# Issuing a branch's transfers from GpSimd instead of SyncE, and storing one of the two split output chunks whole

## The chip, the cores and the metric

The kernel runs on one core of a Trainium2 chip. Its engines are TensorE (PE; its weight loads are PEld), VectorE (DVE), ScalarE (ACT), GpSimd (POOL) and SyncE (SP). A q behind a name (SPq, POOLq) is that engine's sequencer, which waits, branches and issues transfers. The metric is the device time of one execution in microseconds (us), less is better. Before the change the median of three runs is 294.77 us (294.74 to 294.92).

## What is computed

```
x   = attention(q, k, v, s)          # 8 batches, 8 heads, 576 positions, width 64
#     scores = q k^T / 8 + min(-(cum_i - cum_j), 0), causal, softmax; cum = cumsum(max(s, 0))
h   = relu(x^T w_tok1) w_tok2        # token mixing, 576 -> 256 -> 576
u   = x + h^T
out = u + relu(u w_ch1) w_ch2        # channel mixing, 512 -> 1536 -> 512; float32
```

## The kernel before

The fast path assumes that the inputs stay in a range in which the softmax needs no row maximum. While it runs it computes a flag that says whether this held (`flagi`, line 1364). At its end all five engines load the flag (line 1399) and branch on it (line 1402). Where the flag is 0, as with these inputs, they jump over `general`, a slow and safe version of the whole computation in a loop over the batches; the profile has no row of `general`.

On the fast path the work is a list of operations with costs, priorities and dependences. A planner (`Plan.run`) walks it once, gives each operation an engine and a start, and the instructions are then written out in the order of those starts; each engine runs its own list in that order. The cores of the work per batch `b` are `quad` and `pair` (attention), `tok` (token mixing) and `chan` (channel mixing).

`chan(b, ...)` first makes `g`, the hidden layer, and then the output in chunks of 128 positions. For each chunk, 12 matmuls (line 1261) sum `wc2` against `g` into one of four accumulators `pmx`, VectorE adds `u` (line 1269) into one of four output buffers `of`, and SyncE stores it (line 1274). `whole` (line 1255) says whether a chunk is made in one piece of 512 columns or in two of 256; it is false for chunk 3 (`NJ - 2`) of the last two batches, 6 and 7. In `ga` lies the hidden layer of an even batch, in `gb` that of an odd one. The planner puts the last chunks of batch 7 (from `gb`) ahead of the last three of batch 6 (from `ga`), so that the last store of the program is one of batch 6.

Each transfer raises a semaphore when it has landed. Those issued by SyncE go round eight of them, DMAHW0 to DMAHW7, those issued by GpSimd round another eight, DMASW0 to DMASW7. Where the two sides of the branch meet again, the side that was taken must have raised every semaphore as far as the other side would have: the skipping side therefore waits for its own count on each semaphore that `general` uses and adds what `general` would have added. After that come line 1429, where SyncE waits for all engines and all sixteen queues in twelve instructions of two semaphores each (the DMASW ones first, then DMAHW0 to DMAHW7 in turn, each beside an engine's), and a closing barrier. In the profile line 1402 holds the branch and that adding up, line 1429 the closing waits, and line 1418 the opening ones.

Of the kernel before, what the change touches and what calls it, by code (L numbers as in the profile page):

```python
# [262 lines left out]
def c_pe(n, f32=False):  # L263
    occ = n * (4 if f32 else 1) / 2400.0 + 0.0025
    return occ, occ + 0.21
# [17 lines left out]
def general(ctx, tc, q, k, v, out, cum, ident, w1, w2, wc1, wc2):  # L283

    nc = tc.nc
    B, H, S, D = q.shape
    NJ, DM, NCC = 5, H * D, wc2.shape[1]
    AX = mybir.AxisListType.X
    scr = tc.dram_tile([B * H, S], FP32, name="scr")
    with tc.tile_pool(name="gen", bufs=1) as gp, tc.tile_pool(name="gen2", bufs=2) as g2, \  # L290
            tc.tile_pool(name="genp", bufs=1, space=bass.MemoryType.PSUM) as pp:
        nc.sync.dma_start(out=scr[:, :], in_=cum[:, :])
        with tc.For_i(0, B, 1) as b:
            x = gp.tile([128, NJ, DM], BF16, name="gx", tag="gx")
            alln = []
            for i, src in enumerate((q, k, v)):
                f = g2.tile([128, NJ, H, D], FP32, name="gf", tag="gf")
                nc.vector.memset(f[64:128, NJ - 1, :, :], 0.0)
                for c in range(NJ):
                    n = min(128, S - c * 128)  # L300
                    nc.sync.dma_start(
                        out=f[0:n, c, :, :],
                        in_=src[bass.ds(b, 1), :, c * 128 : c * 128 + n, :].rearrange("o h p d -> p (o h) d"))
                t = gp.tile([128, NJ, H, D], BF16, name="gn", tag=f"gn{i}")
                nc.vector.tensor_copy(out=t[:, :, :, :], in_=f[:, :, :, :])
                alln.append(t)
            cb = gp.tile([128, H, S], FP32, name="gcb", tag="gcb")
            nc.sync.dma_start(
                out=cb[:, :, :], in_=scr[bass.ds(b * H, H), :].unsqueeze(0).to_broadcast([128, H, S]))
            for h in range(H):  # L310
                nat = [t[:, :, h, :] for t in alln]
# [51 lines left out]
            for c in range(NJ):  # L363
# [7 lines left out]
                for m in range(4):  # L371
# [3 lines left out]
                                      in_=pt[:, :].rearrange("p (m t) -> p m t", m=4))  # L375
# [8 lines left out]
            for c in range(NJ):  # L384
                n = min(128, S - c * 128)
                pm = pp.tile([128, DM], FP32, name="gpm", tag="gpm")
                for cc in range(NCC):
                    nc.tensor.matmul(out=pm[:, :], lhsT=g[:, cc, c * 128 : c * 128 + 128], rhs=wc2[:, cc, :],
                                     start=(cc == 0), stop=(cc == NCC - 1))
                o = g2.tile([128, DM], FP32, name="go", tag="go")  # L390
                nc.vector.tensor_tensor(out=o[:, :], in0=pm[:, :], in1=u[:, c, :], op=ALU.add)
                nc.sync.dma_start(out=out[bass.ds(b, 1), c * 128 : c * 128 + n, :].rearrange("o p d -> (o p) d"),
                                  in_=o[0:n, :])


# [1 line left out]
def kernel(  # L397
# [12 lines left out]
    nc = tc.nc  # L410

    B, H, S, D = q.shape
# [3 lines left out]
    NJ = 5  # L416
# [17 lines left out]
    def sb(name, shape, dt, pool=None):  # L434
        return (pool or const).tile(shape, dt, name=name, tag=name)
# [124 lines left out]
    cum = sb("cum", [64, S], FP32)  # L560
# [7 lines left out]
    def dve(n, fn, two=False):  # L568
        return {"DVE": (*c_dve(n, two), fn)}
# [15 lines left out]
    for ti, src in enumerate((k, q)):  # L585
# [4 lines left out]
        for f in range(2):  # L590
            def cast0(eng, ti=ti, f=f):
# [4 lines left out]
                else:  # L596
# [9 lines left out]
        out=cum[:, :], data0=one_sb[:, 0:1].to_broadcast([64, S]), data1=s_sb[:, :], initial=0.0, op0=ALU.mult, op1=ALU.add))},  # L606
        reads=["sr"], writes=["cum"], prio=2)
    P.op(dve(1, lambda: nc.vector.tensor_scalar(
        out=half[:, :], in0=cum[:, S - 1 : S], scalar1=-0.5, scalar2=None, op0=ALU.mult)),
        reads=["cum"], writes=["half"], prio=-1)  # L610
    P.op(act(576, lambda: nc.scalar.activation(
        out=wn[:, 0:S], in_=cum[:, :], func=AF.Exp, bias=half[:, 0:1], scale=1.0), True),
        reads=["half", "cum"], writes=["wn"], prio=-5)
    P.op({"ACT": (1.0, 1.1, lambda: nc.scalar.copy(out=neg[:, :, :],
                                                   in_=zero[:, :].unsqueeze(1).to_broadcast([128, 2, 512])))},
# [602 lines left out]
    def chan(b, u, us, uT):  # L1218
        P.shift = SHIFT["chan"][b]
        odd = b % 2  # L1220
        rank = 4 * (b + 1) + LAG
        g = Buf(r_gb if odd else r_ga)
        spans = [(0, 256), (256, 640)] if b == 1 else [(0, 320), (320, 640)] if odd else [(0, 256), (256, 512)] if b == 0 else [(0, 512)]
        for (cc, (a, e)) in ([(cc, sp) for hf in range(2) for sp in spans for cc in range(6 * hf, 6 * hf + 6)] if b < 2 else
                             [(cc, sp) for cc in range(NCC) for sp in spans]):
            if True:
                ukeys = ([(uT, c, m) for c in range(2) for m in range(NMC)] if b < 1 and a == 0 else
                         [(uT, c) for c in range(a // 128, (e + 127) // 128)])
                pm = Buf(r_mx, False)
                n = e - a  # L1230

                def mm(cc=cc, pm=pm, a=a, e=e):
                    for m in range(NMC):
                        nc.tensor.matmul(out=pm.t[:, 0 : e - a], lhsT=wc1[:, m, cc * 128 : cc * 128 + 128],  # L1234
                                         rhs=uT.t[:, m, a:e], start=(m == 0), stop=(m == NMC - 1))
                P.op({"PE": (4 * c_pe(n)[0], 4 * c_pe(n)[0] + 0.21, mm)},
                     reads=ukeys + [("wc1", cc // (NCC // 2) * 2 + m) for m in range(2)],
                     writes=[(pm, 0)],
                     holds=[g], prio=(rank + (cc // 6 + 0.05 * (cc % 6) + 0.4 * (a > 0) if b < 2 else 2.0 * cc / NCC), 0)).late = 2.0
                P.op(either(n,  # L1240
                            lambda cc=cc, pm=pm, a=a, e=e: nc.scalar.activation(  # L1241
                                out=g.t[:, cc, a:e], in_=pm.t[:, 0 : e - a], func=AF.Relu),
                            lambda cc=cc, pm=pm, a=a, e=e: nc.vector.tensor_scalar_max(
                                out=g.t[:, cc, a:e], in0=pm.t[:, 0 : e - a], scalar1=0.0)),
                     reads=[(pm, 0)], writes=[(g, cc, a)], prio=0)
        if b == B - 1:
            P.writer["last"] = P.ops[-2]
        for ci, c in enumerate((4, 0, 1, 2, 3) if odd else (0, 1, 2, 3)):
            if odd:
                src, si = (us, 0) if c == NJ - 1 else (u, c)  # L1250
            else:
                src, si = u, c
            sk = [(us, 0, 0), (us, 0, 64)] if src is us else [(u, si, 0)]
            o = Buf(r_o, False)
            whole = b < B - 2 or c != NJ - 2
            for (na, ne) in ([(0, DM)] if whole else [(0, DM // 2), (DM // 2, DM)]):
                pm = Buf(r_mx, False)
                for th in range(3):
                    def mm(c=c, pm=pm, th=th, na=na, ne=ne):
                        for cc in range(th * 4, th * 4 + 4):  # L1260
                            nc.tensor.matmul(out=pm.t[:, na:ne], lhsT=g.t[:, cc, c * 128 : c * 128 + 128],  # L1261
                                             rhs=wc2[:, cc, na:ne], start=(cc == 0), stop=(cc == NCC - 1))
                    occ = 4 * c_pe(ne - na)[0]
                    P.op({"PE": (occ, occ + 0.21, mm)},
                         reads=[(g, cc, a) for cc in range(th * 4, th * 4 + 4) for (a, e) in spans] + [("wc2", i) for i in range(th * 4 // 3, (th * 4 + 3) // 3 + 1)],
                         writes=[(pm, 0)], holds=[o], prio=(rank + 2.0 + 2.0 * ci / NJ, 1 + (na > 0)))

                def add(pm=pm, o=o, src=src, si=si, na=na, ne=ne):
                    nc.vector.tensor_tensor(out=o.t[:, na:ne], in0=pm.t[:, na:ne], in1=src.t[:, si, na:ne], op=ALU.add)  # L1269
                P.op(dve(ne - na, add), reads=[(pm, 0)] + sk, writes=[(o, na)], prio=0)  # L1270

                def st(o=o, c=c, na=na, ne=ne):
                    if c < NJ - 1:
                        nc.sync.dma_start(out=out[b, c * 128 : c * 128 + 128, na:ne], in_=o.t[:, na:ne])
                    else:
                        for i in range(2):
                            nc.sync.dma_start(out=out[b - 1 + i, NQ:S, :], in_=o.t[i * 64 : i * 64 + 64, :])
                P.op({"SP": (0.6 if c < NJ - 1 else 1.2, 0, st)}, reads=[(o, na)], prio=0, dma=128 * 0.088 / 16)
# [40 lines left out]
    for b in range(B):  # L1319
# [29 lines left out]
        out=pre[:, :], data0=one_sb[:, 0:1].to_broadcast([64, S]), data1=wn[:, 0:S], initial=0.0, op0=ALU.mult, op1=ALU.add))},  # L1349
# [5 lines left out]
        out=bad[:, 4:], in0=sq[:, :], scalar1=16.0, scalar2=None, op0=ALU.is_gt)),  # L1355
# [14 lines left out]
    for o in [o for o in order if o.eng == "PE"]:  # L1370
# [3 lines left out]
        while t1 - t0 > 0.1:  # L1374
            n = min(512, max(128, int((t1 - t0) * 2400)))
# [5 lines left out]
            if not slots:  # L1381
# [4 lines left out]
                out=t[:, 0:n], lhsT=zero[:, 0:128], rhs=zero[:, 0:n], start=True, stop=True)  # L1386
# [47 lines left out]
```

## Time and profile before

| | |
|---|---|
| median of 3 runs | 294.77 us (294.74 to 294.92) |
| the profiled execution | 294.16 us |
| its span, first to last instruction | 292.0 us |
| granted TensorE clock, mean | 0.995 |
| busy: PE, PEld, DVE, ACT, POOL | 282.1, 166.4, 192.0, 188.5, 99.6 us |
| last VectorE addition starts | 286.98 us |
| last store issued | 287.43 us |

The profiled execution has 2.16 us outside its span, and its time is 0.6 us under the median of the unprofiled runs. Starts are counted from the first instruction. A row of a line's instructions gives a count, the shortest, median and longest duration in ns, and the first and last start.

### The profile page before, as it was taken

Reading aid. Unit: us, or ns where it says so; the run is one execution under the profiler, and the core shown is the slowest. Engines: PE = TensorE matmul, PEld = TensorE weight load, DVE = VectorE, ACT = ScalarE, POOL = GpSimd, SP = SyncE. Lnnn points to the kernel's source line nnn. Section 1 sums busy time; section 2 is a strip of 40 time slices with the busy share of each in tenths; the row PEclk is TensorE's granted clock in tenths of the full one; section 3 lists DMA queues with packets and bytes.
Section 4 is the critical chain, followed back from the end, with each engine's and each line's share of the span. In section 5 each row is a group of like instructions: output and inputs, shape, how many; then the busy total and the mean of one; then the engine's idle time right before and its main releaser. Section 6 shows DMA issues by size and latency. Waiting matters only on the chain.

```text
span 292.0 us, 6909 instructions
## 1 busy us (share of the span) xinstructions
PE 282.1 (97%) x2734; PEld 166.4 (57%) x2769; DVE 192.0 (66%) x419; ACT 188.5 (65%) x300; POOL 99.6 (34%) x193
## 2 busy tenths in 40 slices
PE   8999999999999999999999999999999999999993
PEld 3567765676755554457764554556655544575552
DVE  5984779999999758779799956463346468201221
ACT  5786987879999377179897244987452559474000
POOL 8745678756600840029700093510004300000000
PEclk9999999999999999999999999999999999999997
DMA  7999999999935793249976699493616992300332
GB/s 222 225 206 206 206 212 252 189 239 173 208 59 113 135 272 60 72 128 139 188 121 125 109 167 150 93 215 75 160 23 113 195 245 47 86 0 4 109 108 79
DMA packets 66070, 41.82 MB, mean 143 GB/s; under 512 B 47248, under 2 KB 58832, under 8 KB 66032
## 3 DMA queue, kind: packets, MB, share of 16 engines
q0 software_dynamic: 34672, 24.39, 53.7%
q1 hardware_dynamic: 31360, 16.93, 24.3%
q8 instruction: 23, 0.38, 0.5%
q14 instruction: 15, 0.12, 0.1%
HBM read 40.91 MB, written 9.44 MB: 172 GB/s over the span
## 4 chain that ended last, share of the span: by engine, by line
PE 93%; DVE 3%; issue 1%; ACT 1%; DVEq 0%
PE pmx L1234 32%; PE pmx L1261 32%; PE pmx L1115 6%; PE pmx L1177 6%; PE psc L1013 5%; PE psc L926 4%; PE pmx L1385 2%; PE pmx L852 2%; PE psc L917 2%; PE psc L903 1%; DVE kq L875 1%; ACT x L1035 1%; PE pmx L1202 1%; PE psc L852 0%; DVE ua L1184 0%
## 5 line engine op out<-in xcount | busy, mean ns | idle before, releaser
L950 ACT ACTIVATE E<-psc 128x1024 bf16<-128x1024 f32 x64 | 62.1, 1022 | 33.2 <-PE psc L926 23.8
L1234 PEld LDWEIGHTS <-wc 128*128 128x128 bf16 x624 | 58.9, 98 | 31.8 <-issue 0.3
L1234 PE MATMUL pmx<-uTb,wc 128*128 128x320 bf16 (+2 forms) x384 | 55.9, 299 | 0.1
L1261 PE MATMUL pmx<-wc,gb 128*128 128x512 bf16 (+1 forms) x241 | 54.6, 369 | 0.8 <-issue 0.3
L1234 PE MATMUL pmx<-uTa,wc 128*128 128x512 bf16 (+1 forms) x235 | 44.3, 336 | 0.2
L1261 PE MATMUL pmx<-wc,ga 128*128 128x512 bf16 (+1 forms) x195 | 43.5, 366 | 0.6 <-issue 0.2
L1241 ACT ACTIVATE gb<-pmx 128x320 bf16<-128x320 f32 (+2 forms) x66 | 28.9, 438 | 14.1 <-PE pmx L1234 9.1
L1261 PEld LDWEIGHTS <-gb 128*128 128x128 bf16 x252 | 23.6, 98 | 24.2
L685 POOL DMA_DIRECT2D vf<-in_v_dram x39 | 33.6, 872 | 4.5 <-issue 2.1
L1241 ACT ACTIVATE ga<-pmx 128x512 bf16<-128x512 f32 (+1 forms) x36 | 19.0, 534 | 17.8 <-PE pmx L1234 17.3
L1261 PEld LDWEIGHTS <-ga 128*128 128x128 bf16 x204 | 19.1, 98 | 18.9
L719 ACT ACTIVATE junk<-qkn 128x1152 bf16<-128x1152 bf16 x24 | 28.0, 1166 | 0.4
L959 DVE TENSOR_TENSOR E<-E,keep 128x512 bf16<-128x512 bf16 x56 | 22.1, 417 | 8.5 <-ACT E L950 8.4
L703 DVE TENSOR_TENSOR vp<-vf,wT 128x512 bf16<-128x512 f32 (+1 forms) x39 | 25.4, 681 | 0.2
L1013 PEld LDWEIGHTS <-E 128*128 128x128 bf16 x576 | 21.4, 97 | 5.2
L1046 DVE TENSOR_TENSOR x<-psc,rc 128x640 bf16<-128x640 f32 x28 | 22.9, 820 | 0.7
L875 DVE COPY kq<-pmx 128x576 bf16<-128x576 bf16 x27 | 19.8, 750 | 4.8 <-PE pmx L852 4.2
L1269 DVE TENSOR_TENSOR of<-pmx,ua 128x512 f32<-128x512 f32 (+1 forms) x17 | 11.2, 659 | 17.5 <-PE pmx L1261 17.5
L1269 DVE TENSOR_TENSOR of<-pmx,ub 128x512 f32<-128x512 f32 (+1 forms) x17 | 11.2, 658 | 15.5 <-PE pmx L1261 15.5
L1013 PE MATMUL psc<-vp,E 128*128 128x65 bf16 x522 | 20.8, 193 | 0.1
L1115 PE MATMUL pmx<-x,w 128*128 128x512 bf16 (+2 forms) x119 | 19.4, 307 | 0.3 <-issue 0.2
L1177 PE MATMUL pmx<-h,w 128*128 128x512 bf16 x75 | 19.3, 379 | 0.3
(127 smaller groups left out, 322.3 us busy)
## 6 DMA issues: line engine op xcount, KB each, us to landing
vf<-in_v_dram POOLq DMA_DIRECT2D x32, 256.0 KB, 6.4
out_dram<-of SPq DMA_DIRECT2D x30, 256.0 KB, 2.4
qkn<-in_k_dram POOLq DMA_DIRECT2D x15, 288.0 KB, 6.2
qkn<-in_q_dram POOLq DMA_DIRECT2D x15, 288.0 KB, 7.6
wc<-in_moe_w_ch_dram POOLq DMA_DIRECT2D x8, 384.0 KB, 8.3
out_dram<-of SPq DMA_DIRECT2D x12, 128.0 KB, 2.3
qkn<-in_k_dram POOLq DMA_DIRECT2D x9, 128.0 KB, 5.4
qkn<-in_q_dram POOLq DMA_DIRECT2D x9, 128.0 KB, 5.5
```

Of the source, the lines that this page charges most:

```text
L685: nc.gpsimd.dma_start(out=vf.t[p0 : p0 + n, c, :, :], in_=v[b, :, c * 128 : c * 128 + n, :].rearrange("h p d -> p h d"))
L703: eng.tensor_tensor(out=vp.t[p0 : p0 + n, c, :, 0:D], in0=vf.t[p0 : p0 + n, c, :, :], in1=wT[p0 : p0 + n, cw, b * H : b * H + H].unsqueeze ...
L719: nc.scalar.activation(out=junk[:, :].rearrange("p (t n) -> p t n", t=2), in_=i, func=AF.Square, accum_out=sq[:, col : col + 1])
L875: nc.vector.tensor_copy(out=o, in_=i)
L950: nc.scalar.activation(out=E.t[:, :, 512 * pc : 512 * pc + 512], in_=ps.t[:, :].rearrange("p (e n) -> p e n", e=2), func=AF.Exp, scale=0.125)
L1013: nc.tensor.matmul(out=o[:, ic, 0:DE], lhsT=E.t[:, hh, d0 : d0 + 128], rhs=vp.t[:, jc, h + hs_ * hh, 0:DE], start=(jc == j_lo), stop=(jc = ...
L1046: nc.vector.tensor_tensor(out=(x.t[:, :, :].rearrange("p c (m e d) -> p m e c d", e=2, d=D)[:, h // 2] if late else x.t[:, :, :].rearrange ...
L1115: nc.tensor.matmul(out=cols(pm.t[:, :], ha, hb), lhsT=w1[:, NJ if odd and c == NJ - 1 else c, t * 128 : t * 128 + 128], rhs=cols(x.t[:, c, ...
L1177: nc.tensor.matmul(out=pm.t[:, :], lhsT=w2[:, t, w0 : w0 + 128], rhs=h1.t[:, t, :], start=(t == 0), stop=(t == NTC - 1))
L1234: nc.tensor.matmul(out=pm.t[:, 0 : e - a], lhsT=wc1[:, m, cc * 128 : cc * 128 + 128], rhs=uT.t[:, m, a:e], start=(m == 0), stop=(m == NMC ...
L1241: lambda cc=cc, pm=pm, a=a, e=e: nc.scalar.activation(out=g.t[:, cc, a:e], in_=pm.t[:, 0 : e - a], func=AF.Relu),
L1261: nc.tensor.matmul(out=pm.t[:, na:ne], lhsT=g.t[:, cc, c * 128 : c * 128 + 128], rhs=wc2[:, cc, na:ne], start=(cc == 0), stop=(cc == NCC - 1))
```

## The change

Every transfer in `general` is issued by GpSimd, where SyncE did it: the copy of `cum` to `scr`, the loads, the load of `cb`, the stores. And `whole` becomes true for batch 7: only chunk 3 of batch 6 stays split.

```
@@ general
-        nc.sync.dma_start(out=scr[:, :], in_=cum[:, :])
+        nc.gpsimd.dma_start(out=scr[:, :], in_=cum[:, :])
...
-                    nc.sync.dma_start(
+                    nc.gpsimd.dma_start(
                         out=f[0:n, c, :, :],
...
-            nc.sync.dma_start(
+            nc.gpsimd.dma_start(
                 out=cb[:, :, :], in_=scr[bass.ds(b * H, H), :].unsqueeze(0).to_broadcast([128, H, S]))
...
-                nc.sync.dma_start(out=out[bass.ds(b, 1), c * 128 : c * 128 + n, :].rearrange("o p d -> (o p) d"),
+                nc.gpsimd.dma_start(out=out[bass.ds(b, 1), c * 128 : c * 128 + n, :].rearrange("o p d -> (o p) d"),
                                   in_=o[0:n, :])
@@ chan
-            whole = b < B - 2 or c != NJ - 2
+            whole = b != B - 2 or c != NJ - 2
```

SyncE's last stores and its branch, with the semaphore that each store waits for and then raises (`of0_100` holds chunk 3 of batch 7, the three buffers behind it the last three chunks of batch 6):

```order
-L1274 DMA out_0_dram<-of0_100 128x256 [waits DMAHW3_49,DVE_49]
-L1274 DMA out_0_dram<-of0_100 128x256 [waits DMAHW4_49,DVE_49]
-L1274 DMA out_0_dram<-of1_101 128x512 [waits DMAHW5_49,DVE_49]
-L1274 DMA out_0_dram<-of2_102 128x512 [waits DMAHW6_49,DVE_49]
+L1274 DMA out_0_dram<-of0_100 128x512 [waits DMAHW3_49,DVE_49]
+L1274 DMA out_0_dram<-of1_101 128x512 [waits DMAHW4_49,DVE_49]
+L1274 DMA out_0_dram<-of2_102 128x512 [waits DMAHW5_49,DVE_49]
+L1274 DMA out_0_dram<-of3_103 128x256 [waits DMAHW6_49,DVE_49]
 L1274 DMA out_0_dram<-of3_103 128x256 [waits DMAHW7_49,DVE_49]
-L1274 DMA out_0_dram<-of3_103 128x256 [waits DMAHW0_49,DVE_49]
 L1402 COMPARE_AND_BRANCH
```

One store falls away, so that the last one moves from DMAHW0 to DMAHW7; chunk 3 of batch 6 is still stored in two pieces, last of all.

The end of `general` on SyncE, where it meets the skipping side (the last row is the branch past the join; the rows of line 392 are `general`'s stores):

```order
-L392 ISA
-L392 DMA out_0_dram<-go_5321 64x512 [waits DMAHW6_49,DMAHW5_49,DVE_49]
 L293 REGISTER_ALU
 L293 COMPARE_AND_BRANCH
 L293 UNCONDITIONAL_BRANCH [waits DMASW5_49,DMASW4_49,DMASW6_49,DMASW3_49,DMASW7_49,DMASW2_49,DMAHW0_49,DMASW1_49,DMAHW1_49,DMASW0_49,DMAHW2_49,SP_sequencer_49,DMAHW3_49,DVE_sequencer_49,DMAHW4_49,PE_sequencer_49,DMAHW5_49,Activation_sequen
-L1402 UNCONDITIONAL_BRANCH [waits DMAHW0_49,DMAHW1_49,DMAHW2_49,DMAHW3_49,DMAHW4_49,DMAHW5_49,DMAHW6_49,DMAHW7_49]
+L1402 UNCONDITIONAL_BRANCH
```

SyncE has nothing left to add up at the join.

The same place on GpSimd:

```order
+L392 ISA
+L392 DMA out_0_dram<-go_5307 64x512 [waits DMASW2_49,DMASW1_49,DVE_49]
 L293 REGISTER_ALU
 L293 COMPARE_AND_BRANCH
 L293 UNCONDITIONAL_BRANCH [waits DMASW5_49,DMASW4_49,DMASW6_49,DMASW3_49,DMASW7_49,DMASW2_49,DMAHW0_49,DMASW1_49,DMAHW1_49,DMASW0_49,DMAHW2_49,SP_sequencer_49,DMAHW3_49,DVE_sequencer_49,DMAHW4_49,PE_sequencer_49,DMAHW5_49,Activation_sequen
-L1402 UNCONDITIONAL_BRANCH [waits Pool_49]
+L1402 ISA [waits Pool_49,DMASW4_49,DMASW5_49,DMASW3_49,DMASW6_49,DMASW2_49,DMASW7_49,DMASW1_49,DMASW0_49]
+L1402 UNCONDITIONAL_BRANCH
 L1429 ISA [waits barrier_Pool_Activation_PE_DVE_SP_gather]
```

The adding up of eight semaphores, now the DMASW ones, stands on GpSimd. Beside this, four register moves at the program's start (line 1418), which transfers at addresses computed at run time need, pass from SyncE's list to GpSimd's.

## Prediction, made before the changed kernel ran

> **What bounds the kernel now.** I read the page first, then the chain of waits, the instructions in order of time at the end, and the rows of lines 1402, 1429 and 1418, which hold the branch, the closing waits and the opening ones.
>
> ```profile
> span 292.0 us, 6909 instructions
> PE 282.1 (97%) x2734; PEld 166.4 (57%) x2769; DVE 192.0 (66%) x419; ACT 188.5 (65%) x300; POOL 99.6 (34%) x193
> PE 93%; DVE 3%; issue 1%; ACT 1%; DVEq 0%
> ```
>
> TensorE is busy 97% of the span and is 93% of the chain that ended last. Work taken off any other engine inside that chain is worth nothing. But the change touches no working instruction of the first 276 us; it touches the start, the last chunks and what follows them. So I look at the end.
>
> ```profile
> 276.56 0.69 DVE L1269 TENSOR_TENSOR of<-pmx,ub 128x512 f32<-128x512 f32 x1 [1.84 <-PE pmx L1261]
> 277.87 0.42 DVE L1269 TENSOR_TENSOR of<-pmx,ub 128x256 f32<-128x256 f32 x1 [0.62 <-PE pmx L1261]
> 279.18 0.42 DVE L1269 TENSOR_TENSOR of<-pmx,ub 128x256 f32<-128x256 f32 x1 [0.89 <-PE pmx L1261]
> 281.77 0.69 DVE L1269 TENSOR_TENSOR of<-pmx,ua 128x512 f32<-128x512 f32 x1 [2.17 <-PE pmx L1261]
> 284.36 0.69 DVE L1269 TENSOR_TENSOR of<-pmx,ua 128x512 f32<-128x512 f32 x1 [1.90 <-PE pmx L1261]
> ...
> 286.98 0.42 DVE L1269 TENSOR_TENSOR of<-pmx,ua 128x256 f32<-128x256 f32 x1 [0.89 <-PE pmx L1261]
> 287.43 0.33 SPq L1274 DMA_DIRECT2D out_dram<-of  x1
> ```
>
> The last addition ends at 287.40 and its store is issued at 287.43. The span ends at 292.0, so 4.6 us lie behind all arithmetic. The view of transfers in the window from 287.4 on says when that store has landed:
>
> ```profile
> out_dram<-of SPq DMA_DIRECT2D x1, 128.0 KB, 1.9
> ```
>
> 287.4 + 1.9 = 289.3. Then come the rows of lines 1402 (whole) and 1429 (between 289.3 and 290.74):
>
> ```profile
> L1402 SPq EVENT_SEMAPHORE  x8: 17/17/17, 289.3 to 289.9; - x8
> L1402 ACTq COMPARE_BRANCH  x1: 50/50/50, 267.0 to 267.0; - x1
> L1402 POOLq COMPARE_BRANCH  x1: 45/45/45, 267.0 to 267.0; - x1
> L1402 POOLq EVENT_SEMAPHORE  x1: 17/17/17, 267.5 to 267.5; - x1
> L1402 ACTq EVENT_SEMAPHORE  x1: 17/17/17, 269.7 to 269.7; - x1
> L1402 PEldq COMPARE_BRANCH  x1: 3842/3842/3842, 285.4 to 285.4; - x1
> L1402 DVEq COMPARE_BRANCH  x1: 72/72/72, 287.6 to 287.6; - x1
> L1402 SPq COMPARE_BRANCH  x1: 58/58/58, 287.8 to 287.8; - x1
> L1402 DVEq EVENT_SEMAPHORE  x1: 21/21/21, 288.2 to 288.2; - x1
> L1402 PEldq EVENT_SEMAPHORE  x1: 51/51/51, 289.3 to 289.3; - x1
> L1429 SPq EVENT_SEMAPHORE  x12: 28/28/28, 289.9 to 290.6; - x12
> L1429 SPq DRAIN  x2: 7/10/13, 290.7 to 290.7; - x2
> ```
>
> This is the tail. SyncE branches at 287.8 and stands until 289.3, when the last store lands: that store raises DMAHW0, and DMAHW0 is the first of the eight semaphores that SyncE adds up. So all eight of those instructions (289.3 to 289.9) and all twelve closing waits (289.9 to 290.7) come after the landing, one by one, 0.06 to 0.08 us each. Only then does SyncE reach the barrier, and the barrier takes the rest:
>
> ```profile
> L1429 POOLq EVENT_SEMAPHORE  x4: 17/17/17, 290.8 to 291.9; - x4
> L1429 POOLq EVENT_SEMAPHORE_RANGE_CLEAR  x1: 177/177/177, 291.1 to 291.1; - x1
> ```
>
> GpSimd leaves its wait at 290.8, clears, and the span ends at 292.0: 1.3 us that the change leaves alone. None of this is busy time; no share of engines shows it.
>
> **The change, part by part.**
>
> *The adding up leaves SyncE.* With no transfer of `general` on SyncE there is nothing to add: 8 instructions, 289.9 - 289.3 = 0.6 us, all on the path. GpSimd takes up the adding for its eight queues. It branches at 267.0 and goes on at 267.5, more than 20 us before anyone needs it; even if it paid several us there, nothing would move. If that cover were gone, it would cost the same 0.6.
>
> *The last store raises DMAHW7 instead of DMAHW0.* This comes from the whole chunk: one store fewer turns the round by one. Among the twelve closing waits DMAHW7 stands in the last. SyncE can now enter the list right after its branch, at about 288.3 (GpSimd and VectorE went on 0.5 and 0.6 us after theirs), and pass eleven waits in 11 x 0.064 = 0.7 us (0.064 being (290.6 - 289.9) / 11), by 289.0, while the store is still on its way. What is late next is TensorE: it comes back from its branch only at 289.3, adds its count in 51 ns, and SyncE's eleventh wait pairs DMAHW6 with TensorE's semaphore. So the eleventh goes through at 289.4, the twelfth at 289.45 (the store has landed at 289.3), two drains of 0.07 each follow: 289.6 against 290.74. Both parts together: **-1.15 us**, of which 0.6 for the adding up and 0.55 for eleven closing waits slipping under the landing, less what TensorE holds back. If TensorE held nothing, it would be 0.1 more.
>
> *Whole chunk 3 of batch 7.* 24 matmuls of 256 columns become 12 of 512. The additions above show the price: two halves took (277.87 - 276.56) + (279.18 - 277.87) = 2.62 us, a whole chunk 281.77 - 279.18 = 2.59. **-0.03 us**, on TensorE's path. The whole chunk is added in 0.69 instead of 0.42 twice and stored later, but two more chunks of 2.59 and two halves follow before the end, so its buffer, its accumulator and its store are covered by 7.8 us of matmuls.
>
> *Four register moves go from SyncE to GpSimd at the start.*
>
> ```profile
> L1418 SPq MOVE  x4: 29/34/42, 0.0 to 0.2; - x4
> L1418 POOLq EVENT_SEMAPHORE  x2: 17/17/17, 0.6 to 0.6; - x2
> L1418 POOLq INC_SWDGE_SEM  x1: 31/31/31, 0.1 to 0.1; - x1
> L1418 SPq DRAIN  x1: 7/7/7, 0.3 to 0.3; - x1
> L1418 POOLq DRAIN  x1: 192/192/192, 0.3 to 0.3; - x1
> L1418 SPq EVENT_SEMAPHORE  x1: 17/17/17, 0.7 to 0.7; - x1
> ```
>
> The opening barrier opens when GpSimd is through: its drain runs from 0.3 to 0.5, it releases at 0.6, and SyncE goes on at 0.7 and issues the first load. SyncE itself was ready at 0.3, so what it sheds is worth nothing. On GpSimd the four moves stand ahead of the drain, and everything in the program starts behind it. Their price lies between their bare duration, 4 x 0.034 = 0.14, and SyncE's own pace, 0.3 us from the first move to the drain. SyncE's pace is the nearer row, the same four moves at the same place, but read to a tenth only; I take **+0.2 us**.
>
> *The moved transfers.* No row of `general` is in the trace. Issuing them elsewhere costs nothing in this execution, and GpSimd's list for the fast path has no new row.
>
> Sum on the profiled execution: 294.16 - 1.15 - 0.03 + 0.2 = 293.18. Its time lies 0.6 under the median of the runs (294.77), so I apply the difference, -0.98, to the median: **293.8 us**.
>
> [...] The rows show what a jump costs here: GpSimd went on 0.5 us after its branch, VectorE 0.6, ScalarE 2.7 (267.0 to 269.7), TensorE 3.8. [...] The second rival prices a slow jump from the rows alone.
>
> **The rivals.**
>
> *TensorE's return decides more than I allow.* Before, it came back at 289.3 together with the landing, and 1.4 us of SyncE's waits followed, so a late return was hidden. Now each 0.1 us of it counts. Its branch took 3.84 us against ScalarE's 2.7; 15% more is 0.58, and 294.77 - 0.98 + 0.58 = 294.4. From 1 us on the gain is gone. [...] Against it: nothing about TensorE's list behind 279 us changes. Chance 0.12, counted as no change.
>
> *An engine's jump that was quick becomes slow: slower than before.* The lists shift, by one instruction on VectorE and by several on SyncE, and the skipped `general` on SyncE shrinks. If SyncE's target were no longer at hand, it would go on 2.7 us after 287.8, at 290.5, then twelve waits (0.7) and the drains (0.14): 291.35 instead of 290.74, +0.6; with +0.2 - 0.03 that is 295.55. On VectorE the same would bring it back at 290.3 and the drains at 290.55: -0.2 + 0.2 = 294.8. It decides from the point at which the return passes 289.4. Against it: SyncE's jump gets shorter, and a quick one over the longer `general` was quick enough (back by 289.3 at the latest). [...] Chance 0.08, slower.
>
> *The change does other than its words.* If chunk 3 of batch 6, the last of all, were the one stored whole, the last addition would take 0.69 instead of 0.42 and the gain would be 0.27 smaller, 294.1. The order of SyncE's stores excludes it: two stores of 256 columns still stand last. Chance 0.
>
> **How the numbers follow.** A measurement of this kernel tells about 0.2%, 0.59 us, from no change. My forecast, 0.98, is beyond it: chance 0.75. The late TensorE has 0.12, the slow jump 0.08, and 0.05 is left for what I do not see, 0.02 for no change and 0.03 for slower. So faster 0.75, same 0.14, slower 0.11. The range: at its low end TensorE holds nothing (0.1), the moves cost 0.14, and the runs spread 0.15: 293.4. At its high end lie the late TensorE and VectorE's slow jump: 294.8. SyncE's slow jump and the unknown stay outside.
>
> **What would show it.** In the profile after: no SPq row at line 1402 but the branch; SyncE's twelve waits starting at about 288.3 instead of 289.9, the last two at about 289.4; some six POOLq instructions at line 1402 near 267 instead of two; the closing barrier 1.1 to 1.2 us earlier; GpSimd's four moves at line 1418 and its first release at about 0.8 instead of 0.6; the chunk from `gb` with 12 matmuls and one addition of 0.69. The span may lose some 0.1 more, since SyncE's moves no longer mark its start. I am wrong if SyncE's closing waits still all follow the landing, if TensorE's return is past 290, or if the opening release moves by more than 0.4 us.

## The result, and the profile after

The changed kernel takes 293.12 us (median of 8 runs, 292.92 to 293.81). The kernel before, run beside it, takes 294.52 (8 runs, 294.13 to 294.92). The ratio is 0.9955, with a 95% interval of 0.9943 to 0.9968: 1.3 us, or 0.45%, faster. The sign of the forecast was right. The size was not: 0.98 was forecast, and 293.12 lies under the range's low end of 293.4.

The profiled execution took 293.0 us, with a span of 291.2. This is its page, the head and the chain that ended last:

```profile
span 291.2 us, 6914 instructions
PE 284.3 (98%) x2757; PEld 165.3 (57%) x2757; DVE 191.5 (66%) x418; ACT 188.5 (65%) x300; POOL 101.3 (35%) x193
PE 94%; DVE 2%; DMA 1%; ACT 1%; issue 0%; DVEq 0%
```

TensorE bounds the kernel as it did before, so the gain has to lie at the ends. These are VectorE's instructions in order of time (start, duration):

```profile
276.95 0.69 DVE L1269 TENSOR_TENSOR of<-pmx,ub 128x512 f32<-128x512 f32 x1 [1.84 <-PE pmx L1261]
279.54 0.69 DVE L1269 TENSOR_TENSOR of<-pmx,ub 128x512 f32<-128x512 f32 x1 [1.90 <-PE pmx L1261]
282.13 0.69 DVE L1269 TENSOR_TENSOR of<-pmx,ua 128x512 f32<-128x512 f32 x1 [1.90 <-PE pmx L1261]
...
287.34 0.42 DVE L1269 TENSOR_TENSOR of<-pmx,ua 128x256 f32<-128x256 f32 x1 [0.89 <-PE pmx L1261]
```

The chunk that is now whole takes 279.54 - 276.95 = 2.59 us, as worked out. But the last addition starts at 287.34, 0.36 *later* than before (286.98), and the span still ends 0.8 earlier. So the stretch from the last addition to the end lost 1.1 us (5.04 before, 3.90 now). The rows of line 1402 show what became of the branch:

```profile
L1402 POOLq EVENT_SEMAPHORE  x5: 17/42/43, 270.0 to 270.4; - x5
L1402 POOLq COMPARE_BRANCH  x1: 45/45/45, 267.4 to 267.4; - x1
L1402 POOLq INC_SWDGE_SEM  x1: 460/460/460, 270.5 to 270.5; - x1
L1402 PEldq COMPARE_BRANCH  x1: 3838/3838/3838, 285.8 to 285.8; - x1
...
L1402 SPq COMPARE_BRANCH  x1: 58/58/58, 288.2 to 288.2; - x1
...
L1402 PEldq EVENT_SEMAPHORE  x1: 51/51/51, 289.7 to 289.7; - x1
```

SyncE has no row there but its branch: the adding up stands on GpSimd, which jumps at 267.4 and goes on at 270.0: 2.6 us where it was 0.5, about what ScalarE took before (2.7), and hidden, as GpSimd's part in the closing barrier starts only at 290.4. Next, SyncE at line 1429, in the windows 288 to 289.3 and 289.3 to 290.3:

```profile
L1429 SPq EVENT_SEMAPHORE  x10: 27/28/28, 288.4 to 289.0; - x10
...
L1429 SPq EVENT_SEMAPHORE  x2: 28/237/446, 289.3 to 289.8; - x2
L1429 SPq DRAIN  x1: 123/123/123, 290.2 to 290.2; - x1
```

Ten closing waits pass while the last store is on its way, as forecast. The eleventh starts at 289.3, when the last store but one has landed, and takes 446 ns, for TensorE (back at 289.7); the twelfth follows at 289.8. Then comes something that no step of the prediction has: the drain stands only at 290.2, 0.4 us behind the last wait (0.07 before), and takes 123 ns (13 before). And GpSimd at line 1429, first of the kernel before (its other rows are quoted above), then of the changed one:

```profile
L1429 POOLq DRAIN  x2: 107/150/192, 290.9 to 291.6; - x2
```

```profile
L1429 POOLq EVENT_SEMAPHORE  x4: 17/17/17, 290.4 to 291.1; - x4
L1429 POOLq DRAIN  x2: 46/76/107, 290.6 to 291.0; - x2
L1429 POOLq EVENT_SEMAPHORE_RANGE_CLEAR  x1: 178/178/178, 290.8 to 290.8; - x1
```

Before, from clearing to second drain it was 291.1 to 291.6, and that drain took 192 ns; now it is 290.8 to 291.0 and 46 ns. The closing barrier, 1.25 us before (290.76 to 292.01), takes 0.80 (290.44 to 291.24); the expectations below put it at 0.77. Last, the opening:

```profile
L1418 POOLq MOVE  x4: 29/29/39, 0.2 to 0.4; - x4
L1418 POOLq EVENT_SEMAPHORE  x2: 17/17/17, 0.8 to 0.9; - x2
```

The release comes at 0.86 instead of 0.64, the 0.2 that was put down for it.

### The profile page after: what moved, and what is told of

Read it like the earlier page. It is cut to its first block, busy times and chain, and to the rows that moved or that the text cites. A ratio compares the mean times of both kernels' runs of the same rounds, so it can differ in the third digit from the quotient of the medians.

```text
span 291.2 us, 6914 instructions
## 1 busy us (share of the span) xinstructions
PE 284.3 (98%) x2757; PEld 165.3 (57%) x2757; DVE 191.5 (66%) x418; ACT 188.5 (65%) x300; POOL 101.3 (35%) x193
## 4 chain that ended last, share of the span: by engine, by line
PE 94%; DVE 2%; DMA 1%; ACT 1%; issue 0%; DVEq 0%
PE pmx L1234 33%; PE pmx L1261 33%; PE pmx L1177 6%; PE pmx L1115 6%; PE psc L1013 5%; PE psc L926 4%; PE pmx L852 2%; PE psc L917 2%; DMA gb<-in_k_dram 1%; PE psc L903 1%; PE pmx L1385 1%; ACT x L1035 1%; PE pmx L1202 1%; DVE kq L875 0%; PE psc L852 0%; DVE x L1029 0%
## 5 line engine op out<-in xcount | busy, mean ns | idle before, releaser
L1261 PE MATMUL pmx<-wc,gb 128*128 128x512 bf16 x240 | 55.6, 379 | 0.0
L1234 PE MATMUL pmx<-uTa,wc 128*128 128x512 bf16 (+1 forms) x240 | 44.9, 337 | 0.0
L1261 PE MATMUL pmx<-wc,ga 128*128 128x512 bf16 (+1 forms) x204 | 44.6, 367 | 0.0
L1261 PEld LDWEIGHTS <-gb 128*128 128x128 bf16 x240 | 22.4, 98 | 25.1
L1269 DVE TENSOR_TENSOR of<-pmx,ub 128x512 f32<-128x512 f32 x16 | 11.0, 689 | 16.0 <-PE pmx L1261 14.0
## 6 DMA issues: line engine op xcount, KB each, us to landing
qkn<-in_k_dram POOLq DMA_DIRECT2D x15, 288.0 KB, 6.3
qkn<-in_q_dram POOLq DMA_DIRECT2D x15, 288.0 KB, 6.7
```

## The experiments

In the table, "release" is GpSimd's at the opening. "Tail" runs from the start of the last addition to GpSimd's wake at the closing barrier, "barrier" from there to the end of the span; starts are the trace's, to 0.01 us. "Outside" is the mean, over all runs, of the time less the span. Its scatter within a kernel is 0.02 to 0.06.

| kernel | median us (runs) | ratio to before, 95% | release | tail | barrier | outside |
|---|---|---|---|---|---|---|
| before | 294.52 (24) | 1 | 0.64 | 3.79 | 1.25 | 2.19 |
| changed | 293.12 (8) | 0.9943-0.9968 | 0.86 | 3.10 | 0.80 | 1.80 |
| a2_again | 293.34 (6) | 0.9950-0.9976 | 0.86 | 3.14 | 0.80 | 1.78 |
| e1_issue_only | 293.74 (11) | 0.9966-0.9983 | 0.86 | 3.29 | 0.80 | 1.97 |
| e2_whole_only | 293.57 (6) | 0.9960-0.9984 | 0.64 | 3.49 | 1.25 | 1.99 |
| e3_opening | 294.20 (11) | 0.9984-1.0002 | 0.86 | 3.77 | 0.80 | 1.95 |
| p1_gpsimd_shift | 294.31 (11) | 0.9982-1.0004 | 0.64 | 3.76 | 0.79 | 2.16 |
| p2_synce_shift | 292.77 (5) | 0.9925-0.9952 | 0.86 | 2.64 | 0.80 | 1.76 |
| p3_whole_synce_shift | 293.78 (8) | 0.9966-0.9987 | 0.64 | 3.23 | 1.25 | 1.98 |
| p4_whole_vectore_shift | 294.10 (11) | 0.9969-0.9990 | 0.64 | 3.32 | 1.25 | 2.11 |
| p5_tensore_hint | 293.92 (12) | 0.9966-0.9994 | 0.86 | 3.91 | 0.80 | 1.63 |
| p7_synce_shift8 | 292.97 (6) | 0.9936-0.9965 | 0.86 | 2.59 | 0.79 | 1.78 |
| e4_scalare_whole | 293.83 (10) | 0.9967-1.0010 | 0.64 | 3.28 | 1.10 | 2.01 |
| p8_two_hints | 292.45 (6) | 0.9913-0.9945 | 0.86 | 2.49 | 0.80 | 1.64 |

The kernel before stands at 294.4 to 294.7 beside each group. What is left, from release to last addition, is TensorE's and differs from profile to profile (286.2 to 288.0 us, without order), so medians of a few runs carry some 0.3 us of it. The columns don't, but for one thing: the tail holds the last store's own time, which lands 2.28 to 2.40 us after the last addition starts, and 2.57 and 2.59 us after it in the traces of e2 and p5.

**The two parts apart, and the opening by itself.** `e1_issue_only` makes only the first part of the change (transfers on GpSimd), `e2_whole_only` only the second.

```
e1:  nc.sync.dma_start -> nc.gpsimd.dma_start (all of general); whole as before
e2:  whole = b != B - 2 or c != NJ - 2; general as before
```

> The first part alone: general's transfers on GpSimd, and chunk 3 of batch 7 still stored in two pieces, so that the last store raises DMAHW0 as before. Theory of serial waits: SyncE adds nothing up (-0.6 us) and passes the four DMASW waits ahead of the landing (-0.25), the remaining eight follow it; the opening is 0.22 later: together about -0.6. If the closing barrier (1.25 us in the kernel before, 0.77 in the changed one) is shorter because of what GpSimd now has at the join, it is shorter here too, and the total is about -1.1. Rival, the barrier's length differs by execution and not by kernel: it may come out anywhere between 0.77 and 1.25 here.

> The second part alone: chunk 3 of batch 7 stored whole, general's transfers still on SyncE, so that the last store raises DMAHW7, the last of the eight semaphores that SyncE adds up. Theory of serial waits: seven of the eight additions pass while the store is on its way (-0.5 us), all twelve closing waits still follow the landing, the whole chunk is worth -0.03, the opening is unchanged: about -0.5. The closing barrier stays at about 1.25 if its shortening came with GpSimd's new list; if it is about 0.8 here too, the new list has nothing to do with it. Rival, the gain was one part's only: 0 here, or all 1.3.

Each part brings about half. The first: 0.77 us by the ratio (0.5 to 1.0), and its barrier is short, 0.80. The second: 0.82 (0.5 to 1.2), barrier 1.25. So the short barrier goes with the issuing on GpSimd. But e1's tail falls by only 0.50, where 0.85 was expected, and SyncE's rows say why (windows 289.9 to 290.2 and 290.2 to 290.7):

```profile
L1429 SPq EVENT_SEMAPHORE  x3: 27/28/28, 289.9 to 290.0; - x3
...
L1429 SPq EVENT_SEMAPHORE  x2: 28/28/28, 290.4 to 290.5; - x2
L1429 SPq DRAIN  x2: 7/10/13, 290.6 to 290.7; - x2
```

Here is the 0.4 us step again, between the tenth and the eleventh wait (290.0 to 290.4), with nothing left to wait for; the last store had landed at 289.7. In the changed kernel it stands two instructions later. SyncE's list is two instructions shorter there: the store that fell away and its wait. e2's tail falls by 0.29, where 0.5 was expected: its last store lands 0.25 later behind the addition than before (2.57 against 2.32). p3 below, the same kernel with two drains more, lands it after 2.31 and has a tail shorter by 0.55. Of e2's total, 0.20 lies outside the span.

`e3_opening` is the kernel before with only part of `general`'s transfers on GpSimd, enough to bring the four moves (`i` is 0 for the loads of q).

```
-                    nc.sync.dma_start(
+                    (nc.sync if i else nc.gpsimd).dma_start(
...
-                nc.sync.dma_start(out=out[...
+                nc.gpsimd.dma_start(out=out[...
```

> The kernel before with only general's first loads and its output stores on GpSimd, the other load and the copy of cum left on SyncE: four register moves stand on GpSimd ahead of the opening barrier as in the changed kernel, but SyncE still adds up all eight DMAHW semaphores behind the last store. This is the opening's cost by itself: the release at 0.86 instead of 0.64 us, and if nothing else changes, a time 0.22 us above the kernel before. If the closing barrier is shorter because GpSimd now adds up eight semaphores at the join, the time is 0.5 lower than that, about -0.3 against before. Rival, a late opening is absorbed by the first loads: 0.

Its total is 0.2 us lower, not clear of no change (-0.5 to +0.06): release 0.86, tail as before, barrier 0.80. And outside the span it has 0.24 less.

> The changed kernel once more, for a second trace and five more rounds: 1.3 us faster than before (0.9 to 1.7). By the theory that the closing barrier's length belongs to the kernel, it takes 0.77 us again; by the rival that it differs by execution, it takes something else between 0.7 and 1.3. The same for the 0.38 us in which SyncE stood between its last closing wait and its drain: again there by a theory of the kernel, gone by chance.

The step ahead of SyncE's drain (0.41 us, drain 122 ns) and the short barrier are there again: they belong to the kernel, not to one execution. The total was 1.1 us below before (0.7 to 1.5).

**Where the list is cut.** A step that keeps its place in the list and waits for nothing suggests the list itself. The page of the changed kernel shows transfers of instructions during the run (queue, number, MB):

```profile
q8 instruction: 23, 0.38, 0.6%
q14 instruction: 16, 0.13, 0.2%
```

They come in pieces of 0.13 / 16 MB, about 8 KB, and 0.38 / 23 MB, about 16 KB. The theory then: an engine that passes from one piece to the next stands 0.3 to 0.4 us, even when its next instruction needs nothing. The test is to lengthen a list and see whether the step moves by just as many instructions.

```
 p1 (on the kernel before):         p2 (on the changed kernel):      p7: 8 drains instead of 4
+for _ in range(5):                 +for _ in range(4):
+    nc.gpsimd.drain()              +    nc.sync.drain()
```

The drains stand where the engine is idle: GpSimd's behind its last transfer, SyncE's between two of its last stores.

> The kernel before with five drains more on GpSimd, behind its last transfer and ahead of its branch at 267 us, where it idles for 20 us; nothing else changes. Theory of the list's edge: an engine that passes from one block of its instruction list to the next stands 0.3 to 0.4 us, and a drain right behind that edge is longer by some 0.1. In the kernel before GpSimd's edge falls between its clearing and its last drain, inside the closing barrier (0.52 us from one to the other against 0.21, and the drain 192 ns against 46); five instructions more put it ahead of the barrier, where GpSimd waits anyway. So the closing barrier takes 0.77 instead of 1.25, and the time falls by 0.45 to 0.5; if the 0.22 by which the time outside the span is shorter in every kernel with the new GpSimd list comes from there too, by 0.7. Rival, the barrier is shorter because GpSimd has added up eight semaphores ahead of it, not because of where its list is cut: barrier 1.25, time 0.

GpSimd at line 1433, the former 1429:

```profile
L1433 POOLq EVENT_SEMAPHORE  x4: 17/17/17, 291.6 to 292.3; - x4
L1433 POOLq DRAIN  x2: 38/72/107, 291.8 to 292.2; - x2
L1433 POOLq EVENT_SEMAPHORE_RANGE_CLEAR  x1: 177/177/177, 292.0 to 292.0; - x1
```

The clearing at 292.0 is followed by the drain at 292.2, 38 ns long. The barrier takes 0.79 with no semaphore added up on GpSimd, so the rival falls. The total, 0.2 us lower by the ratio (-0.5 to +0.1), does not settle the 0.46 by itself. Outside the span it has 2.16, so the cut in GpSimd's list has nothing to do with the 0.22 there.

> The changed kernel with four drains more on SyncE between two of its last stores, where it waits for VectorE. Theory of the list's edge: the step of 0.40 us ahead of SyncE's drain (and the drain of 123 ns instead of 13) moves four instructions forward, between the eighth and the ninth closing wait, which pass while the last store is on its way; the drain follows the twelfth wait after 0.07, and the end comes 0.45 us earlier than in the changed kernel: 292.7 to 292.8. What is late then is TensorE's return at 289.7. Rival, the step belongs to the drain, which cannot pass until some 0.6 us after the last store has landed: it stays at the drain, and the time is that of the changed kernel, 293.2.

SyncE of p2 (windows 288 to 289.1 and 289.1 to 290.05), and behind it of p7 (288 to 288.5 and 288.5 to 289.7):

```profile
L1433 SPq EVENT_SEMAPHORE  x8: 28/28/28, 288.4 to 288.9; - x8
...
L1433 SPq EVENT_SEMAPHORE  x4: 28/28/342, 289.3 to 289.9; - x4
L1433 SPq DRAIN  x2: 7/7/7, 289.9 to 290.0; - x2
```

> The changed kernel with eight drains more on SyncE instead of four. By the theory of the list's edge the step of 0.40 us moves another four instructions forward, between the fourth and the fifth closing wait, and the total is that of four drains, 292.8, since both places lie ahead of the landing. By the rival that four drains at that place helped for another reason (SyncE arriving later at the closing waits), the step stays between the eighth and the ninth.

```profile
L1433 SPq EVENT_SEMAPHORE  x4: 28/28/28, 288.1 to 288.3; - x4
...
L1433 SPq EVENT_SEMAPHORE  x8: 28/28/317, 288.7 to 289.5; - x8
L1433 SPq DRAIN  x2: 7/7/7, 289.5 to 289.6; - x2
```

The step stands behind the eighth wait with four drains and behind the fourth with eight: four instructions for four, to the instruction. Counted through an engine's whole list in program order, with the skipped instructions of `general`, the step stands behind SyncE's 210th instruction in all five kernels that have it (changed, a2, e1, p2, p7), and behind GpSimd's 454th in the kernel before and in e4 below. In p2 and p7 it runs while the last store is on its way, and the drain follows the last wait at once, 7 ns long. The tail is 2.64 and 2.59 against 3.10. The totals go the same way, 292.77 in p2, as expected, and 292.97 in p7, but their intervals overlap that of the changed kernel; it is the rows that show the move.

**What lies outside the span.** It fell from 2.19 to 1.80, which the prediction did not count at all.

```
 p3 (on e2):                        p4 (on e2):                      e4 (on e2):
+for _ in range(2):                +nc.vector.drain()                nc.sync.dma_start -> nc.scalar.dma_start
+    nc.sync.drain()                                                 (all of general)
```

> The second part alone with two drains more on SyncE between its last stores, so that SyncE's list is as long as in the kernel before. This looks for the 0.2 us by which the time outside the span fell with the second part (2.19 before, 1.99 with the second part alone). If SyncE's list, two instructions shorter, is the cause (an edge past the last recorded instruction), the time outside the span is 2.19 again and the total is 0.2 above the second part alone, 293.8; if not, it stays at 1.99 and the total at 293.6. The span itself should not change by more than 0.1.

> The second part alone with one drain more on VectorE some 5 us ahead of its last addition, so that VectorE's list is as long as in the kernel before (the second part takes one addition out). The same question as in the run beside it, for VectorE: outside the span 2.19 and 293.8 if its list is the cause, 1.99 and 293.6 if not. If neither run brings the 0.2 back, it is TensorE's list, 24 instructions shorter, or something that no list explains.

> general's transfers on ScalarE instead of GpSimd, and chunk 3 of batch 7 stored whole: the four register moves stand on ScalarE, which is 0.4 us early at the opening barrier, and the eight additions stay on SyncE. The opening is as in the kernel before, first release at 0.64; the closing barrier is 1.25, since GpSimd's list is that of the kernel before; the end as with the second part alone, so that the total is 293.6. It tells what the 0.22 outside the span that went with the four moves on GpSimd is: 1.99 here if it went with GpSimd's moves (or what they delay), 1.77 if it went with SyncE losing its moves.

By the time outside the span, SyncE's list is not it (1.98 in p3). The totals of p3 and p4 (293.78 and 294.10) don't tell: their intervals overlap that of e2. One instruction more on VectorE brings back 0.12 of the 0.20 that the second part took (2.11). With the moves on ScalarE it is 2.01, so the other 0.22 goes with moves on GpSimd: every kernel that has them there lies 0.2 lower than its like without. e4's release (0.64) and its 2.01 are as expected; its total, 293.83, is not clear of the kernel before. Its barrier is not as expected, 1.10 where 1.25 was put down.

```profile
L1429 POOLq EVENT_SEMAPHORE  x4: 17/17/17, 290.6 to 291.6; - x4
L1429 POOLq DRAIN  x2: 50/78/107, 290.8 to 291.4; - x2
L1429 POOLq EVENT_SEMAPHORE_RANGE_CLEAR  x1: 177/177/177, 291.2 to 291.2; - x1
```

Here the step (290.8 to 291.2) stands ahead of the clearing instead of behind it. I had taken GpSimd's list for that of before; in the skipped `general` it has one instruction more (138 in the loop's body, not 137), and the cut moves by one. The stretch of 0.30 remains, and the drain, no longer right behind the cut, takes 50 ns instead of 192.

**TensorE's return.** In p2 the eleventh wait takes 342 ns, for TensorE. A hint for its branch was tried on p2, then a second one on VectorE. The line stands in the kernel without engines, and leaves no hint in any list of the fast path then.

```
 p5:  tc.mark_branch_hint_location("general", "LikelyTaken", engines=[mybir.EngineType.PE])
 p8:  tc.mark_branch_hint_location("general", "LikelyTaken", engines=[mybir.EngineType.PE, mybir.EngineType.DVE])
```

> The changed kernel with the four drains on SyncE, and with a hint at the head of TensorE's list that names its branch at the end. What is late in the shifted kernel is TensorE's return: its branch takes 3.84 us and SyncE's eleventh closing wait stands 0.34 us for it. If the hint makes TensorE fetch the far side in time, it returns before 288, the eleventh wait passes with the landing of the last store but one, the twelfth with that of the last, and the end is 0.1 to 0.15 us earlier than in the shifted kernel, 292.65; it cannot be more, since the last store lands at 289.7. Rival: a hint 2700 instructions ahead of the branch does nothing: 3.84 us again, 292.8.

Line 1406 (the former 1402) of p5:

```profile
L1406 PEldq COMPARE_BRANCH  x1: 398/398/398, 286.1 to 286.1; - x1
L1406 PEldq EVENT_SEMAPHORE  x1: 51/51/51, 287.6 to 287.6; - x1
L1406 DVEq COMPARE_BRANCH  x1: 72/72/72, 288.2 to 288.2; - x1
L1406 SPq COMPARE_BRANCH  x1: 58/58/58, 288.4 to 288.4; - x1
L1406 DVEq EVENT_SEMAPHORE  x1: 21/21/21, 291.2 to 291.2; - x1
```

The hint does what was hoped for: TensorE is back 1.6 us after its branch (286.06 to 287.62) instead of 3.9. But VectorE, back after 0.58 us in all kernels so far, now comes back 3.0 us after its branch, and SyncE's tenth closing wait stands 1.7 us for it. The total is 293.92, 1.15 above p2. VectorE's own list is as long as in p2.

> The kernel with the hint on TensorE and a second hint, on VectorE. With TensorE's hint alone TensorE came back 1.6 us after its branch instead of 3.9, but VectorE's return, quick in every other kernel (0.4 us), took 3.0 us, and SyncE stood 1.7 us for it at its tenth closing wait. If VectorE stood for a fetch of its far side, its own hint takes that away: it is back within 1 us, SyncE's closing wait ten passes at once, and the twelfth follows the last landing (2.3 us behind the start of the last addition) directly: 1.3 to 1.5 us less than with TensorE's hint alone, about 292.5, which would be 0.1 to 0.3 under the kernel with four drains on SyncE. Rival: hints move the lists of engines that they do not name, and another quick return becomes slow: 293.5 to 294.

```profile
L1406 DVEq COMPARE_BRANCH  x1: 84/84/84, 288.9 to 288.9; - x1
...
L1406 DVEq EVENT_SEMAPHORE  x1: 21/21/21, 289.5 to 289.5; - x1
```

VectorE is back after 0.6 us, the tail is 2.49, and 292.45 is the lowest median here: 0.7% under the kernel before (0.55 to 0.87%), and 0.3 under p2, where 0.1 to 0.3 was expected, though the intervals of p8 and p2 overlap.

## Why the prediction came out too small

Its steps, one by one, against the traces:

| term | predicted | shown |
|---|---|---|
| adding up and waits (tail) | -1.15 | -0.69 |
| whole chunk | -0.03 | -0.03 in the additions; too small for the totals |
| four moves, inside the span | +0.2 | +0.22 |
| closing barrier | 0 | -0.45 |
| outside the span | 0 | -0.39 |
| sum | -0.98 | -1.34, and -1.33 measured by the ratio |

Two terms that the prediction put at nothing, the closing barrier and the time outside the span, brought 0.84 us and took the result below its range. The tail went the other way: it brought 0.46 less than was worked out. That the sum (-0.98) missed the measured change (-1.33) by only 0.35 us is luck: errors of opposite sign.

**The tail's mechanism was right, its size was not.** The eight additions leave SyncE and the waits slip under the landing, as the rows show, but the sum left out 0.46: the cut in SyncE's list came to lie between the last wait and the drain. Before, SyncE seems to have met that cut in its jump, hidden by the landing: in e2, where the next instruction has nothing to wait for, it comes 0.54 us after the branch, in the changed kernel 0.20. The count of the list bears this out: the jump passes SyncE's 210th instruction in e2, p3, p4 and e4 (0.53 to 0.54 us in each) and ends short of it in the changed kernel, e1, p2 and p7 (0.20). The two kernels with hints don't fit: they should have 0.20 and have 0.53. With the cut moved away (p2) the tail falls by 3.79 - 2.64 = 1.15, the predicted number. So the step of the tail that failed is "two drains of 0.07 each follow": it took the list for an even row of instructions. The second rival had the lists shift, but put the price into the jump, 2.7 us; the jump took 0.20, and the step of 0.41 came behind it, after the twelfth wait.

**"1.3 us that the change leaves alone" was wrong.** GpSimd's instructions in the barrier are the same ones, but its list got longer ahead of them, so its cut no longer fell inside the barrier. p1 moves the cut alone and gets the whole 0.46 there; e4 moves it by one instruction, which takes only the 0.15 of the drain off.

**The time outside the span was taken for a constant.** The prediction worked out the span and applied "the difference, -0.98, to the median". That step left out 0.39, and its cause is known only in part.

**The moves cost what was put down, and it comes back.** The release is 0.22 later, and the time outside the span is 0.22 shorter with the moves on GpSimd. The sizes suggest one thing, the opening merely counted from an earlier point, but the traces don't bear that out: the opening drains of VectorE, ScalarE and TensorE start at 0.1, 0.1 and 0.3 us in both kernels. What grew shorter outside the span stays open. The other 0.20 outside the span goes with the second part; one instruction on VectorE accounts for 0.12 of it.

**TensorE's return** is late next, as forecast, at 289.7 instead of 289.3, because the last stretch began 0.36 later. It costs 0.10 to 0.15: that much the tail of p8, where TensorE is early, is shorter than those of p7 and p2. **The quick jump that becomes slow** did not happen on SyncE or VectorE in the changed kernel (GpSimd's did, hidden), but p5 is that rival made real, with VectorE's 3.0 us. **The base** of 294.77 was the median of three runs; with more runs it is 294.52, and the same steps would have given 293.5, still 0.4 above the result. The range's low end, by its own terms (0.1, 0.06 and 0.15 under 293.8), is 293.5 and not 293.4; from the better base it is 293.2, which the result all but reaches.

A step of 0.4 us at every piece does not show on TensorE. In the changed kernel's trace 152 to 336 of TensorE's recorded instructions start between one transfer of the 16 KB queue and the next (from the first to the last but one, 246 on the mean), and at most 37 of any other engine's, so I take the queue's 23 transfers for TensorE's, whose list has 5522 instructions ahead of its branch. At 0.4 us each they would cost 9 us, more than all of TensorE's idle time (291.2 - 284.3 = 6.9). The pieces of the other queue are 8 KB, and in the closing lists of SyncE and GpSimd, where the next instruction waits for nothing, passing from one to the next costs 0.3 to 0.46 us. Only there is the step shown.

## What to carry to other kernels

Where single instructions of a few tens of ns set the end, count not only which of them go but where each engine's list is cut: adding or removing instructions anywhere ahead, in skipped code too, moves the cut (by four and eight instructions for four and eight drains on SyncE, by one for one skipped instruction on GpSimd here), and moving it into a stretch in which the engine waits anyway was worth 0.46 us of the tail for four idle drains. A prediction about the last microseconds should carry that as a term of plus or minus 0.5 per engine in the closing chain (0.46 on GpSimd and 0.46 on SyncE here), and one for the time outside the span (0.39 here). Read a step between two instructions that wait for nothing as a question about the list, and test it by shifting it.

## What the runs showed of the hardware that was not expected

- The step at a cut: 0.40 to 0.41 us from one SyncE instruction to the next (0.06 otherwise) at four places in five runs, and 0.30 on GpSimd. A transfer of instructions on the 8 KB queue starts 0.62 to 0.66 us after SyncE's step in the changed kernel, e1 and p2. A drain that is the first instruction behind the cut takes 0.11 to 0.15 more (123 ns against 13, 192 against 46).
- A hint at the head of TensorE's list, some 5500 instructions ahead of its branch (2757 matmuls and as many weight loads), shortened the return from 3.9 to 1.6 us, made VectorE's slower (0.6 to 3.0) and moved SyncE's cut ahead of its closing waits, although neither list had changed in length. How a hint on one engine moves another's list stays open.
- The time outside the span differs by kernel, from 1.63 to 2.19 us, with a scatter of 0.06 at most; the two kernels with hints have the least.
